# One build-time schedule for all five engines in a chunk-selecting attention followed by a softplus MLP

## Chip, cores and metric

One core of one Trainium2 chip runs the whole kernel. The metric is device time in microseconds (us) of one execution, as the median of several runs. The core has a matrix engine (PE, with its weight loads shown apart as PEld), a vector engine (DVE), an activation engine (ACT), a general engine (POOL) and a queue engine (SP) that issues transfers. Each engine takes its instructions strictly in the order in which they stand in its queue and waits on semaphores for what other engines or transfers must deliver.

## What is computed

```python
B, H, S, D = 4, 8, 768, 64;  chunk = 32;  nc = 24;  top_k = 6
k_min, k_max = min and max of k over each chunk of 32 keys
ub = sum_d max(q * k_min, q * k_max)            # a bound per query and chunk
ub = where(pos // 32 >= chunk index, ub, -1e9)  # causal, by chunks
sel = the 6 chunks with the largest ub of each query
scores = where(sel and causal, q @ k.T / 8, -1e9)
attn = softmax(scores) @ v                      # (4, 8, 768, 64) -> x: (3072, 512)
h = x @ w_in                                    # 512 -> 2048
g = softplus(h)
out = g @ w_out                                 # 2048 -> 512, float32
```

Inputs are float32; the kernel computes in bfloat16 with float32 accumulation.

## The kernel before

The 3072 rows are cut into 12 **blocks** of 256 queries, three to a batch (block kinds 0, 1 and 2: a block of kind k sees k + 1 key spans of 256). For each block there are two stages.

*Preparation* (`prep_block`): k and q of the block are transposed on PE (L175, L191), ACT copies the transposed k out of PSUM into `kt` (L179), DVE reduces `kt` to chunk maxima and minima (`kx`, L181 and L182) and spreads them into a block-diagonal matrix `bd` (L184). DVE makes the positive and negative parts `qpos`, `qneg` of q (L203, L204); PE multiplies both by `bd` (`ub`, L212, L213, always all 24 chunks), DVE adds a causal mask over all 24 chunks (L217), takes the 8 largest of each of 16 rows (L224), compares with the sixth (`mraw`, L226) and PE transposes the result (`mT`, L236, eight transposes, one for each head pair and half block). The mask rows are copied into spare rows of the operands `qa` and `qt` (L241 to L245), and k into `ka` and `kb` (L197, L198 or L239, L240, from `kt`), so that one score matmul yields score plus mask.

*Attention and MLP*: for each of 4 head pairs, `score_step` makes score tiles `s_ps` (two matmuls, L263 and L265), ACT takes the exponential into `pt` (L267), POOL cuts the diagonal (L271); `av_step` multiplies by v (`o_ps`, L285), DVE normalises (L291, L293); `ot_step` transposes into `x` (L304, L305). Then `h_gen`: 64 matmuls `hp` with w_in (L322) with Exp and Ln on ACT (L324, L326), and `y_gen`: 32 matmuls `y` with w_out (L335), a copy on DVE (L340) and a store on SP (L342).

The order is written out by hand: `run_block` steps through the score tiles of a block, and after each tile `slot` runs pieces of the older attention steps, of the MLP (`mlp_stream`, at a rate per slot), of the next block's preparation (the `agenda`: five pieces at slots 0, 2, 5, 9 and 11 of 16) and of the loads. PSUM is cut into pools: two banks for `s_ps`, one for `o_ps`, two for all transposes and `ub`, two for `hp`, one for `y`.

Loads: the k, q, v of blocks 0 to 2 come as float32 (`load_f32`, queues of SP and, for half of block 0, ACT) and are cast on ACT (L103). From block 3 on POOL's queue casts them in the transfer (`load_cast`, L108, L114). The loads of blocks 0, 1 and 2 are issued one behind the other; w_in is issued on POOL's queue in eight pieces (two column halves by four row blocks, L149) during block 0's score tiles, w_out in four pieces behind it (L155).

```python
    with tc.manual_schedule(engines={ET.Activation, ET.DVE, ET.PE}):
        consts(0)
        ...
        loads.append(load_w_in())
        run_block(0, 0.0)
    for nm in "kqv":
        load_f32(nm, 2, (nc.sync, nc.sync))
    consts(1)
    loads.append(load_w_out())
    run_block(1, 0.8)
```

Of the kernel before, what the change touches and what calls it, by code (L numbers as in the profile page):

```python
# [16 lines left out]


@with_exitstack
def kernel(  # L20
# [9 lines left out]
    nc = tc.nc  # L30
    B, H, S, D = q.shape
    CH = 32
    NCH = S // CH
    TOPK = 6
    NQT = S // 128
    NP = H // 2
    scale = 1.0 / math.sqrt(D)
    NEG = -30000.0 / scale

    d_model, d_ff = moe_w_in.shape  # L40
    KDM = d_model // 128
    KFF = d_ff // 128
    QB = 256
    NT = QB // 128
    NBLK = S // QB
    NCB = QB // CH
    blocks = [(b, blk) for b in range(B) for blk in range(NBLK)]
    NB = len(blocks)

    ctx.enter_context(tc.manual_schedule(engines={ET.Pool, ET.SP}))  # L50
    nc.scalar.preload_act_table_set("natural_log_exp_and_others")

    PS = bass.MemoryType.PSUM
    singles = ctx.enter_context(tc.tile_pool(name="singles", bufs=1))
    f_pool = ctx.enter_context(tc.tile_pool(name="f", bufs=6))
    io_pool = ctx.enter_context(tc.tile_pool(name="io", bufs=3))
    qt_pool = ctx.enter_context(tc.tile_pool(name="qt", bufs=3))
    prep = ctx.enter_context(tc.tile_pool(name="prep", bufs=2))
    pt_pool = ctx.enter_context(tc.tile_pool(name="pt", bufs=3))
    st_pool = ctx.enter_context(tc.tile_pool(name="st", bufs=3))  # L60
    x_pool = ctx.enter_context(tc.tile_pool(name="x", bufs=4))
    g_pool = ctx.enter_context(tc.tile_pool(name="g", bufs=3))
    e_pool = ctx.enter_context(tc.tile_pool(name="e", bufs=3))
    mo_pool = ctx.enter_context(tc.tile_pool(name="mo", bufs=3))
    ps_s = ctx.enter_context(tc.tile_pool(name="ps_s", bufs=2, space=PS))
    ps_o = ctx.enter_context(tc.tile_pool(name="ps_o", bufs=1, space=PS))
    ps_t = ctx.enter_context(tc.tile_pool(name="ps_t", bufs=2, space=PS))
    ps_h = ctx.enter_context(tc.tile_pool(name="ps_h", bufs=2, space=PS))
    ps_y = ctx.enter_context(tc.tile_pool(name="ps_y", bufs=1, space=PS))

    V = [singles.tile([128, NQT, H, D + 1], BF16, name=f"v_{i}") for i in range(2)]
    KA = [singles.tile([128, NP, S], BF16, name=f"ka_{i}") for i in range(2)]
    KB = [singles.tile([128, NP, S], BF16, name=f"kb_{i}") for i in range(2)]
    BD = [singles.tile([128, NP, 2, 2, NCH], BF16, name=f"bd_{i}") for i in range(2)]
    Mraw = [singles.tile([128, NP, NT, 2, 32], BF16, name=f"mraw_{i}") for i in range(2)]
    w_in_sb = singles.tile([128, KDM, d_ff], BF16, name="w_in_sb")
    w_out_sb = singles.tile([128, KFF, d_model], BF16, name="w_out_sb")

    src = {"k": k, "q": q, "v": v}
    xfs, loaded = {}, {}  # L80

    def rows(nm, n, t):
        b, blk = blocks[n]
        r0 = blk * QB + t * 128
        return src[nm][b, :, r0:r0 + 128].rearrange("h s d -> s h d")

    def load_f32(nm, n, eng):
        xf = f_pool.tile([128, NT, H, D], F32, name="xf")
        for t in range(NT):
            eng[t].dma_start(out=xf[:, t], in_=rows(nm, n, t))  # L90
        xfs[nm, n] = xf

    def v_dst(n, t):
        b, blk = blocks[n]
        return V[b % 2][:, blk * NT + t, :, 0:D]

    def cast_f32(nm, n):
        xf = xfs.pop((nm, n))
        if nm != "v":
            loaded[nm, n] = io_pool.tile([128, NT, H, D], BF16, name=nm + "_sb")  # L100
        for t in range(NT):
            dst = v_dst(n, t) if nm == "v" else loaded[nm, n][:, t]
            nc.scalar.copy(dst, xf[:, t])  # L103

    def load_cast(nm, n):
        if nm == "v":
            for t in range(NT):
                nc.gpsimd.dma_start(out=v_dst(n, t), in_=rows(nm, n, t))  # L108
                yield
        else:  # L110
            xb = io_pool.tile([128, NT, H, D], BF16, name=nm + "_sb")
            loaded[nm, n] = xb
            for t in range(NT):
                nc.gpsimd.dma_start(out=xb[:, t], in_=rows(nm, n, t))  # L114
                yield

    for nm in "kqv":
        load_f32(nm, 0, (nc.sync, nc.scalar))

    ident = singles.tile([128, 128], BF16)  # L120
    make_identity(nc, ident)
    ohb = singles.tile([32, S], BF16, name="ohb")
    nc.vector.memset(ohb, NEG)
    cmask = singles.tile([128, NQT, NCH], F32, name="cmask")
    nc.vector.memset(cmask, 0.0)
    nc.gpsimd.affine_select(out=ohb, in_=ohb, compare_op=ALU.is_ge, fill=0.0,
                            base=0, channel_multiplier=-CH, pattern=[[1, S]])
    nc.gpsimd.affine_select(out=ohb, in_=ohb, compare_op=ALU.is_ge, fill=0.0,
                            base=CH - 1, channel_multiplier=CH, pattern=[[-1, S]])
    nc.gpsimd.affine_select(out=ohb, in_=ohb, compare_op=ALU.not_equal, fill=-1.0,  # L130
                            base=-NCH, channel_multiplier=1, pattern=[[0, S]])
    nc.gpsimd.affine_select(out=cmask, in_=cmask, compare_op=ALU.is_ge, fill=-1.0e30,
                            base=0, channel_multiplier=1, pattern=[[128, NQT], [-CH, NCH]])

    for i in range(2):
        nc.vector.memset(Mraw[i], 0.0)

    def consts(i):
        nc.vector.memset(BD[i], 0.0)
        nc.vector.memset(KB[i][0:32], 0.0)  # L140
        nc.vector.memset(V[i][:, :, :, D:D + 1], 1.0)
        nc.sync.dma_start(out=KA[i][64:96], in_=ohb.unsqueeze(1).to_broadcast([32, NP, S]))
        nc.sync.dma_start(out=KB[i][32:64], in_=ohb.unsqueeze(1).to_broadcast([32, NP, S]))

    def load_w_in():
        for half in range(2):
            fs = slice(half * d_ff // 2, (half + 1) * d_ff // 2)
            for kt in range(KDM):
                nc.gpsimd.dma_start(out=w_in_sb[:, kt, fs],  # L149
                                    in_=moe_w_in[kt * 128:(kt + 1) * 128, fs])  # L150
                yield

    def load_w_out():
        for c4 in range(4):
            nc.gpsimd.dma_start(  # L155
                out=w_out_sb[:, c4 * 4:(c4 + 1) * 4, :],
                in_=moe_w_out[c4 * 512:(c4 + 1) * 512, :].rearrange(
                    "(kt ki) f -> ki kt f", ki=128))
            yield

    Q = {}

    def prep_block(n):
        b, blk = blocks[n]
        ka, kb, bd = KA[b % 2], KB[b % 2], BD[b % 2]
        mraw = Mraw[n % 2]
        cs = slice(blk * QB, (blk + 1) * QB)
        cc = slice(blk * NCB, (blk + 1) * NCB)
        early = n < NBLK
        k_sb = loaded.pop(("k", n))  # L170

        kT = ps_t.tile([128, NP, QB], BF16, name="kT", tag="t")
        for t in range(NT):
            for p in range(NP):
                nc.tensor.transpose(kT[:, p, t * 128:(t + 1) * 128],  # L175
                                    k_sb[:, t, 2 * p:2 * p + 2, :], ident)
        kx = prep.tile([128, NP, 2, NCB], BF16, name="kx")
        kt = prep.tile([128, NP, QB], BF16, name="kt")
        nc.scalar.copy(kt, kT)  # L179
        kT4 = kt.rearrange("d p (c g) -> d p c g", g=CH)  # L180
        nc.vector.tensor_reduce(kx[:, :, 0], kT4, axis=AX.X, op=ALU.max)  # L181
        nc.vector.tensor_reduce(kx[:, :, 1], kT4, axis=AX.X, op=ALU.min)  # L182
        for h in range(2):
            nc.vector.tensor_copy(bd[h * 64:(h + 1) * 64, :, :, h, cc], kx[h * 64:(h + 1) * 64])  # L184
        yield

        q_sb = loaded.pop(("q", n))
        qT = ps_t.tile([128, NP, QB], BF16, name="qT", tag="t")
        for t in range(NT):
            for p in range(NP):  # L190
                nc.tensor.transpose(qT[:, p, t * 128:(t + 1) * 128],  # L191
                                    q_sb[:, t, 2 * p:2 * p + 2, :], ident)
        qt = qt_pool.tile([128, NP, QB], BF16, name="qt")
        qa = qt_pool.tile([128, NP, QB], BF16, name="qa")
# [26 lines left out]
        for p in range(NP):  # L221
            for t in range(NT):
                for h in range(2):
                    nc.vector.max(out=m8[:, p, t, h], in_=ub_sb[:, p, t, h])  # L224
# [262 lines left out]
```

## Time and profile before

| | |
|---|---|
| time, 3 runs | 315.68, 315.86, 316.93 us, median 315.86 |
| span of the profiled execution, first to last instruction | 314.1 us |
| the median less that span (start and end of a launch) | 1.8 us |
| busy: PE / PEld / DVE / ACT / POOL | 270.5 / 198.6 / 174.4 / 224.2 / 99.0 us |
| mean granted PE clock | 0.988 |
| moved by DMA | 23.51 MB, mean 75 GB/s |

The page gives no time of its own for the profiled execution besides its span. Busy time is the union of the spans of an engine's instructions. A matmul's span holds the time from its start to its last result, while the next one may start long before, so a row of back-to-back matmuls is read from the starts. In a row of the windows view, the first two numbers are the stretch, then come its length and for each engine the busy time with the number of instructions, the granted PE clock, the mean busy share of the DMA engines, and GB/s.

### The profile page before, as it was taken

How to read it: one execution, taken by the hardware profiler on the slowest of the kernel's cores; microseconds unless marked ns; L12 is line 12 of the kernel's file. 1: busy time of each engine (PE TensorE's matmuls, PEld its weight loads, DVE VectorE, ACT ScalarE, POOL GpSimd, SP SyncE). 2: the span in 40 equal slices, each digit the busy share in tenths (PEclk: the TensorE clock that was granted, in tenths of full speed). 3: DMA queues.
4: the chain of work that ended last, by engine and by line, in shares of the span. 5: the costliest groups of instructions: out<-in, count | busy, mean ns of one | idle time of the engine just before them, and what ended most of it. 6: DMA issues, size and time to landing. Idle time of an engine off the chain costs nothing.

```text
span 314.1 us, 6878 instructions
## 1 busy us (share of the span) xinstructions
PE 270.5 (86%) x2748; PEld 198.6 (63%) x2784; DVE 174.4 (56%) x550; ACT 224.2 (71%) x379; POOL 99.0 (32%) x172
## 2 busy tenths in 40 slices
PE   1335879989899799899999799899999999999983
PEld 0223657667658667677658577677568777776651
DVE  5818582592965964935946946836748732112100
ACT  4578789968837858788628868888539769983550
POOL 4024375622723613514624414424421211111000
PEclk9999959999999999999999999999999999999999
DMA  9999899993933906904913905907900000001101
GB/s 165 200 216 216 147 158 189 92 71 45 80 73 52 83 11 60 101 2 57 90 59 53 83 35 33 102 3 76 94 33 35 3 33 35 2 33 35 67 17 52
DMA packets 82208, 23.51 MB, mean 75 GB/s; under 512 B 75520, under 2 KB 78080, under 8 KB 82176
## 3 DMA queue, kind: packets, MB, share of 16 engines
q0 software_dynamic: 59424, 11.28, 43.9%
q1 hardware_dynamic: 19632, 11.01, 14.3%
q10 hardware_dynamic: 3120, 0.79, 1.4%
q8 instruction: 21, 0.34, 0.4%
q14 instruction: 11, 0.09, 0.1%
HBM read 27.26 MB, written 6.29 MB: 107 GB/s over the span
## 4 chain that ended last, share of the span: by engine, by line
PE 57%; DVE 26%; ACT 12%; issue 2%; DMA 1%; ACTq 0%; DVEq 0%
PE y L335 21%; PE hp L322 17%; PE o_ps L285 5%; PE s_ps L263 4%; DVE kx L181 4%; ACT kt L179 4%; DVE kx L182 4%; PE s_ps L265 3%; PE mT L236 3%; ACT pt L267 2%; DVE qneg L204 2%; ACT e_sb L324 2%; DVE qpos L203 2%; DVE qt L200 2%; DMA xf<-in_k_dram 1%
## 5 line engine op out<-in xcount | busy, mean ns | idle before, releaser
L267 ACT ACTIVATE pt<-s_ps 128x512 bf16<-128x512 f32 (+1 forms) x192 | 103.9, 556 | 36.7 <-PE s_ps L265 29.9
L322 PE MATMUL hp<-x,w_in_sb 128*128 128x256 bf16 x768 | 103.5, 273 | 3.2 <-ACT e_sb L324 1.8
L271 POOL TENSOR_SCALAR_AFFINE_SELECT pt<-pt 128x256 bf16<-128x256 bf16 x96 | 40.9, 426 | 185.5 <-ACT pt L267 185.1
L335 PE MATMUL y<-w_out_sb,g 128*128 128x512 bf16 x348 | 90.7, 379 | 3.6 <-DVE y_sb L340 1.7
L322 PEld LDWEIGHTS <-w_in_sb 128*128 128x128 bf16 x768 | 71.4, 98 | 12.9 <-issue 4.1
L324 ACT ACTIVATE e_sb<-hp 128x512 f32<-128x512 f32 x96 | 58.4, 611 | 27.7 <-PE hp L322 27.4
L335 PEld LDWEIGHTS <-g 128*128 128x128 bf16 x384 | 34.2, 97 | 28.6 <-issue 2.8
L326 ACT ACTIVATE g<-e_sb 128x1024 bf16<-128x1024 f32 x48 | 51.8, 1078 | 0.3
L285 PEld LDWEIGHTS <-pt 128*128 128x128 bf16 x672 | 32.9, 99 | 11.1 <-issue 4.3
L340 DVE COPY y_sb<-y 128x512 f32<-128x512 f32 x24 | 16.5, 687 | 39.7 <-PE y L335 39.5
L291 DVE RECIPROCAL rec<-o_ps 128x4 f32<-128x4 f32 x48 | 8.5, 177 | 38.1 <-PE o_ps L285 37.9
L305 DVE COPY x<-oT 128x256 bf16<-128x256 bf16 x48 | 13.9, 289 | 25.1 <-PE oT L304 24.8
L285 PE MATMUL o_ps<-v_106,pt 128*128 128x65 bf16 x336 | 20.7, 199 | 2.2 <-DVE o_sb L293 1.9
L181 DVE TENSOR_REDUCE kx<-kt 128x32 bf16<-128x1024 bf16 x12 | 14.6, 1219 | 13.0 <-ACT kt L179 13.0
L293 DVE TENSOR_TENSOR o_sb<-o_ps,rec 128x256 bf16<-128x256 f32 x48 | 20.2, 422 | 1.3
L285 PE MATMUL o_ps<-v_107,pt 128*128 128x65 bf16 x336 | 18.4, 193 | 1.7 <-DVE o_sb L293 1.5
L304 PE MATMUL oT<-ident,o_sb 128*128 128x128 bf16 x96 | 13.7, 225 | 4.3 <-DVE o_sb L293 4.3
L114 POOL DMA_DIRECT2D k_sb<-in_k_dram x18 | 16.1, 892 | 0.8 <-issue 0.5
L114 POOL DMA_DIRECT2D q_sb<-in_q_dram x18 | 16.2, 902 | 0.4 <-issue 0.3
L175 PE MATMUL kT<-ident,k_sb 128*128 128x128 bf16 x96 | 8.8, 241 | 8.1 <-ACT k_sb L103 7.6
L263 PE MATMUL s_ps<-qt,kb_110 128*128 128x256 bf16 x48 | 14.0, 293 | 1.6 <-ACT pt L267 0.9
L263 PE MATMUL s_ps<-qa,ka_108 96*128 96x256 bf16 x48 | 14.2, 296 | 0.8 <-DVE qa L241 0.8
(111 smaller groups left out, 365.2 us busy)
## 6 DMA issues: line engine op xcount, KB each, us to landing
out_dram<-y_sb SPq DMA_DIRECT2D x24, 256.0 KB, 2.0
k_sb<-in_k_dram POOLq DMA_DIRECT2D x18, 128.0 KB, 3.8
q_sb<-in_q_dram POOLq DMA_DIRECT2D x18, 128.0 KB, 4.3
w_in_sb<-in_moe_w_in_dram POOLq DMA_DIRECT2D x8, 256.0 KB, 6.9
w_out_sb<-in_moe_w_out_dram POOLq DMA_DIRECT2D x4, 512.0 KB, 9.5
v_107<-in_v_dram POOLq DMA_DIRECT2D x12, 128.0 KB, 5.3
xf<-in_k_dram SPq DMA_DIRECT2D x5, 256.0 KB, 5.1
xf<-in_q_dram SPq DMA_DIRECT2D x5, 256.0 KB, 5.8
```

The costliest lines, as they stand in the source:

```text
L114: nc.gpsimd.dma_start(out=xb[:, t], in_=rows(nm, n, t))
L181: nc.vector.tensor_reduce(kx[:, :, 0], kT4, axis=AX.X, op=ALU.max)
L263: nc.tensor.matmul(s_ps[:, 0:QB], kk[0:nr, p, j * 128:(j + 1) * 128], qq[0:nr, p, :], start=True, stop=True)
L267: nc.scalar.activation(pt[:, h, j:j + 2].rearrange("k j c -> k (j c)")[:, 0:w], s_ps[:, 0:w], ACT.Exp, scale=scale)
L271: nc.gpsimd.affine_select(out=diag, in_=diag, compare_op=ALU.is_ge, fill=0.0, base=0, channel_multiplier=-1, pattern=[[0, 2], [1, 128]])
L285: nc.tensor.matmul(o_ps[:, u, h], pt[:, h, j, c0:c0 + 128], V[b % 2][:, j, 2 * p + h, :], start=(j == 0), stop=(j == t0 + u))
L293: nc.vector.tensor_tensor(o_sb, o_ps[:, :, :, 0:D], rec.to_broadcast([128, NT, 2, D]), op=ALU.mult)
L322: nc.tensor.matmul(hp[:, fi], w_in_sb[:, dt, ft * 128:(ft + 1) * 128], X[n][:, dt], start=(dt == 0), stop=(dt == KDM - 1))
L324: nc.scalar.activation(e_sb[:, f2 * 2:f2 * 2 + 2], hp, ACT.Exp)
L326: nc.scalar.activation(g[:, f4 * 4:(f4 + 1) * 4], e_sb, ACT.Ln, bias=1.0)
L335: nc.tensor.matmul(y, g[:, f, u * 128:(u + 1) * 128], w_out_sb[:, f, :], start=(f == 0), stop=(f == KFF - 1))
L340: nc.vector.tensor_copy(y_sb, y)
```

## The change

The hand-written order is replaced by a graph of operations. Each operation has an engine (some have two to choose from, with a price in ns for each), what it depends on, the buffers that it takes and frees, a due time (`key`), and for loads an earliest time (`rel`) and a `gate`: another transfer that must have landed before it is issued. `Plan.run` simulates the five engines when the kernel is built and places, one after the other, the operation that can start first; among those that can start at the same time on an engine (within `tol` ns) the one with the earliest due time. The order found is then the program order of all five engines, all of which now stand under the manual schedule. The simulation's prices are formulas in the file (`mm`, `act`, `dve`, `LAT`).

With it:
- buffers are single tiles with fixed places that the planner hands out (`sizes`); PSUM has the same eight banks as before, but the transposes of the first two blocks may also take the banks of `h` and `y`;
- w_in is loaded in four column pieces of 512 columns (1 MB of float32 each) gated on the landing of block 1's v; block 2's float32 loads are gated on the third of these pieces, w_out on block 2's v, and everything that comes later on the last piece of w_out; all of the first float32 loads are on SP's queue;
- `ub` has only the 8(k + 1) chunks that a block of kind k can see; the causal mask is added in place, in PSUM, on the four chunks on the diagonal alone; the 8 largest are taken straight from PSUM over those chunks; `mT` takes two head pairs in one transpose (four instead of eight for a block);
- `kt` is gone: DVE reduces the transposed k straight from PSUM, and `ka`, `kb` are copied from PSUM too;
- the minima are negated, so that both parts of q are non-negative; this may run on ACT (Relu);
- blocks 0 and 1 are prepared in two halves of two head pairs each;
- the zeroed rows of the second `kb` and the mask rows of the second `ka`, `kb` come by DMA behind w_out.

The matmuls of scores, v, `hp` and `y` are the same in number and shape. The diff's core (the constants, the operation class, and all code of operations that only changes its form are left out):

```diff
+LAT = {
+    "PE": {"PE": 230, "ACT": 205, "DVE": 205},
+    "ACT": {"PE": 165, "ACT": 145, "DVE": 145, "POOL": 180, "SP": 200},
...
+    def run(self, par):
+        for o in reversed(self.ops):
+            dur = min(c for _, c in o.alts) + (2500 if o.dma else 160)
+            o.due = min([1e12 if o.key is None else o.key] + [s.due - dur for s in o.succ])
+        free = {"PE": 3000.0, "ACT": 2300.0, "DVE": 1000.0, "POOL": 800.0, "SP": 800.0}
...
+            for e, v in cand.items():
+                lim = min(x[0] for x in v) + tol.get(e, 0)
+                x = min((x for x in v if x[0] <= lim), key=lambda x: (x[1].due, x[0], x[1].n))
+                if pick is None or (x[0], x[1].due) < (pick[0], pick[1].due):
+                    pick = (*x, e)
...
+def mm(n):
+    return max(25.0, n / 2.4 + 2.5)
+def act(n, psum=True):
+    return n / 1.2 + (52 if psum else 95)
+def dve(n, rate=1.0):
+    return n / (0.96 * rate) + 66
+PAR = dict(
+    tol={"PE": 1, "ACT": 46, "DVE": 0, "POOL": 0, "SP": 0},
+    alt=39,
...
+    sizes=dict(s=2, h=2, y=1, o=1, t=2, xf=10, io=4, kx=2, q=3, pn=2, ub=2, pt=2, osb=2, x=4, g=3, e=2, ysb=2),
+)
...
+    for i, nm in enumerate("kqv"):
+        load(nm, 0, "f32", 0.1 + 0.6 * i)
+    for i, nm in enumerate("kqv"):
+        load(nm, 1, "f32", 2.0 + 0.6 * i)
+    load_w_in(5.0, [ld["dma", "v", 1, 0]])
+    for i, nm in enumerate("kqv"):
+        load(nm, 2, "f32", 9.0 + 0.6 * i, gate=[w_in[2]])
+    load_w_out(14.0, [ld["dma", "v", 2, 0]])
...
+            def f_kx(e, kT=kT, kx=kx, pp=pp, j=0, t_of=t_of):
+                x = t_of(kT).rearrange("d p (c g) -> d p c g", g=CH)
+                nc.vector.tensor_reduce(kx.ap[:, pp, j], x, axis=AX.X, op=ALU.min if j else ALU.max, negate=bool(j))
...
+                    copy(e, (T.KB if h else T.KA)[i][hs, pp, cs], t_of(kT)[hs])
...
+            C = NCB * (k + 1)
...
+                            nc.vector.max(out=ubs.ap[:, p // 2, t, p % 2, h], in_=x[:, (p - p0) // 2, t, p % 2, h, 0:c])
...
+    need = mybir.DependencyInfo(mybir.DependencyClass.Sync, mybir.DependencyReason.DATA)
+    for o in order:
+        o.inst = o.fn(o.eng)
+        for d in o.gate:
+            tc.add_manual_dep(o.inst.ins, d.inst.ins.name, need, reason="order of loads")
...
-    with tc.manual_schedule(engines={ET.Activation, ET.DVE, ET.PE}):
-        consts(0)
...
-    while later:
-        slot(1.0)
-    for _ in mlp:
-        pass
```

More of the change, by code (lines that the diff above doesn't have):

```diff
@@ new lines, with __init__, ap @@
+LANDED = {"PE": 60, "ACT": 40, "DVE": 40, "POOL": 80, "SP": 80}
+class Pool:
+    def __init__(self, n):
+        self.homes = [None] * n
+        self.ends = [[] for _ in range(n)]
+        self.idle = list(range(n))
+class Buf:
+    __slots__ = ("pools", "pool", "slot", "left", "ends")
+    def __init__(self, *pools):
+        self.pools, self.pool, self.slot, self.left, self.ends = pools, None, None, 0, []
+    @property
+    def ap(self):
+        return self.pool.homes[self.slot]
+class Op:
+    __slots__ = ("name", "alts", "fn", "deps", "gate", "after", "succ", "alloc", "touch", "key",
+                 "rel", "due", "wait", "eng", "start", "end", "done", "dma", "n", "at", "inst")
@@ L77 @@
[L77 to L91, printed above, removed]
```

891 lines of the change are left out of this document (527 added, 364 removed).

## The prediction

> **What bounds the kernel now.** I read the page first (busy times, groups), then PE's timeline for the true spacing of its matmuls, then the windows view to see where PE does less than it could.
>
> ```profile
> PE 270.5 (86%) x2748; PEld 198.6 (63%) x2784; DVE 174.4 (56%) x550; ACT 224.2 (71%) x379; POOL 99.0 (32%) x172
> ...
> L267 ACT ACTIVATE pt<-s_ps 128x512 bf16<-128x512 f32 (+1 forms) x192 | 103.9, 556 | 36.7 <-PE s_ps L265 29.9
> L322 PE MATMUL hp<-x,w_in_sb 128*128 128x256 bf16 x768 | 103.5, 273 | 3.2 <-ACT e_sb L324 1.8
> L335 PEld LDWEIGHTS <-g 128*128 128x128 bf16 x384 | 34.2, 97 | 28.6 <-issue 2.8
> L285 PEld LDWEIGHTS <-pt 128*128 128x128 bf16 x672 | 32.9, 99 | 11.1 <-issue 4.3
> ```
>
> PE is the busiest engine, but 270.5 us counts overlapping spans. PE's timeline gives the spacing from start to start:
>
> ```profile
> 80.32 0.46 PE L285 MATMUL o_ps<-v_106,pt 128*128 128x65 bf16 x10
> 80.62 1.04 PE L322 MATMUL hp<-x,w_in_sb 128*128 128x256 bf16 x8
> ...
> 272.17 1.03 PE L335 MATMUL y<-w_out_sb,g 128*128 128x512 bf16 x4
> 273.03 0.27 PE L263 MATMUL s_ps<-qa,ka_109 96*128 96x256 bf16 x1
> 273.14 0.27 PE L265 MATMUL s_ps<-qa,ka_109 96*128 96x256 bf16 x1
> 273.25 1.04 PE L322 MATMUL hp<-x,w_in_sb 128*128 128x256 bf16 x8
> 274.13 0.27 PE L263 MATMUL s_ps<-qa,ka_109 96*128 96x256 bf16 x1
> 274.24 0.22 PE L265 MATMUL s_ps<-qa,ka_109 96*128 96x128 bf16 x1
> 274.30 0.46 PE L285 MATMUL o_ps<-v_107,pt 128*128 128x65 bf16 x10
> ```
>
> Four `y` in 0.86 us are 215 ns each; eight `hp` in 0.88 are 110; a 128-column matmul takes 60 (I use 56, half of 110); ten `o_ps` in 0.30 are 30. The work is then `hp` 768 x 109 ns = 83.7 us, `y` 384 x 215 = 82.6, scores (two for each of 192 exponentials, 96 of the 384 with 128 columns) 288 x 109 + 96 x 56 = 36.8, `o_ps` 672 x 30 = 20.2. Of the 2784 loads 576 remain: 384 transposes x 56 = 21.5 and 192 bounds of 48 columns, which lie by their columns (21) and the 30 of `o_ps` at some 25 each, 4.8. Together **249.6 us of work in a span of 314.1**: 64.5 us are lost, not the 43.6 that the busy time suggests. (The Trainium skill, "Perfetto Trace Analysis", section Identifying the Most-Contended Engine, calls matmul busy time a bad measure of distance to the limit because matmuls are pipelined; the trace agrees, 270.5 against 249.6.)
>
> Where they are lost, by windows (the last three rows are those of `hp`, `y` and `s_ps` alone):
>
> ```profile
> 60.00:308.70 248.70, 234.52 (x2397) 171.44 (x2429) 140.31 (x433) 178.37 (x307) 75.05 (x126) 1.00 0.46 50
> 60.00:70.00 10.00, 8.60 (x95) 5.92 (x94) 9.78 (x36) 6.91 (x13) 4.82 (x7) 1.00 0.89 57
> 80.00:90.00 10.00, 8.33 (x102) 5.81 (x102) 9.16 (x34) 6.35 (x12) 5.59 (x9) 1.00 1.12 94
> 270.00:300.00 30.00, 29.69 (x261) 20.67 (x264) 5.48 (x14) 19.92 (x34) 2.04 (x5) 1.00 0.10 36
> 0.00:60.00 60.00, 9.59 (x64) 6.22 (x64) 0.94 1.23 180
> 0.00:60.00 60.00, 0.70 (x3) 0.39 (x4) 0.94 1.23 180
> 0.00:60.00 60.00, 12.63 (x56) 0.94 1.23 180
> ```
>
> By 60 us PE has done one block's `hp` (7.0 us), four `y` (0.9), blocks 0 and 1 of attention and part of block 2. A block's attention work with its preparation, by the same spacings, is 4.0, 6.7 and 9.4 us for kinds 0, 1, 2. So some 22 us are done: 38 us lost. From 60 to 308.7 the other 227.5 fill 91.5% of 248.7: 21 us lost. The tail loses 5.4. The middle loss sits where DVE is full: in 60:70 and 80:90 DVE is busy 9.78 and 9.16 of 10 and PE 8.60 and 8.33; with no preparation left (270:300) PE is busy 29.69 of 30.
>
> **The start.** Loads bind it:
>
> ```profile
> 0.00:20.00 20.00, 5.36 (x44) 3.41 (x44) 11.67 (x38) 10.50 (x15) 3.68 (x11) 1.00 1.15 190
> ```
> ```profile
> k_sb<-in_k_dram POOLq DMA_DIRECT2D x18, 128.0 KB, 3.8
> ```
> ```profile
> L322 PE MATMUL hp<-x,w_in_sb x768: 269/272/421, 35.7 to 301.0; 128*128 128x256 bf16 x192
> L335 PE MATMUL y<-w_out_sb,g x348: 376/379/390, 58.6 to 308.3; 128*128 128x512 bf16 x174
> ```
>
> The core moves 190 GB/s. Blocks 0 and 1 are twelve pieces of 256 KB; eleven and the mask rows, about 3.2 MB, land at 17 to 18 us. Then the gate opens: a 128 KB transfer by POOL's queue lands after 3.8 us, of which 0.7 is moving at that rate, so 3.1 is delay; a column piece (512 KB as stored) takes 2.7. The pieces land at about 23, 26, 28.5 and 31. One column piece is enough for the first `hp`, where before one needed a half of w_in: `hp` starts at 23 instead of 35.7. Block 2 follows the third piece; its fifth piece lands at about 36, so w_out's pieces land from 42 to 50, and `y` can start at **42** instead of 58.6. Of PE's work, before 42 there are block 0 (4.0), block 1 (6.7) and two `hp` blocks (14.0), at most 24.7. I take 22, since block 1's exponentials hold back the second `hp`; the low end is 18. From 42 on, block 2's attention, two blocks of `y` and the next `hp` are at hand, so PE is full 18 us earlier with the same work done.
>
> The gates are waits. Behind a gated load on POOL's queue stand diagonal cuts of block 0 and 1, for which `o_ps` waits; the planner knows the wait and sorts by it, so I price this at nothing; if POOL were stuck until a gate opens, block 0's `x` would slip by up to 3 us, still before 23. The casts of blocks 1 and 2 lie beside PE's waiting.
>
> **The parts that change work.** `mT` loses 48 of 96 transposes, 2.7 us of PE: 247.0 remain. DVE, in order:
>
> ```profile
> 80.75 0.68 DVE L200 COPY qt<-qT 128x1024 bf16<-128x1024 bf16 x1
> ...
> 84.42 0.17 DVE L291 RECIPROCAL rec<-o_ps 128x4 f32<-128x4 f32 x1
> 84.51 0.39 DVE L239 COPY ka_109<-kt 64x1024 bf16<-64x1024 bf16 x1
> ...
> 86.26 1.44 DVE L224 MAX8 m_1307<-ub_sb 128x8 f32<-128x24 f32 x16
> ```
>
> `ka` and `kb` cost 0.39 us from SBUF; from PSUM the nearest row is the 0.68 of `qt`: 2 x 0.29 us more in each of nine blocks, 5 us of DVE time beside PE. (The Trainium skill, "VectorE: DVE Perf Modes", section Why PSUM operands drop a tier, says that a PSUM operand keeps DVE out of its fastest copies. It speaks against this edit, and 0.39 against 0.68 agrees.) The sixteen maxima from PSUM are not in the trace: they cost 1.44 us a block now; if each cost as much as the small PSUM read of 0.17, 2.7; if shorter rows halve them, 0.7. I keep 1.44, the same operation. The mask on four chunks instead of 24 saves DVE a little, and ACT loses its copies `kt`. So DVE's work stays near 15 us a block (174.4 / 12 now) against 20.6 of PE (247.0 / 12); what changes is when it is done. Now the five pieces are packed into 12 of 16 slots and fill DVE, so that `o_ps` and `y` (one bank each) wait for their copies. The planner places each operation where it can start and prefers what is due, so most of the 21 us should go. Between 91.5% and the 99% of 270:300 I take 97%, nearer to the latter, because `y` and `hp` of an older block are then ready to fill in, and because two slow DVE steps a block remain.
>
> **The tail** is the same work:
>
> ```profile
> 305.10 3.61 PE L335 MATMUL y<-w_out_sb,g 128*128 128x512 bf16 x16 [0.78 <-DVE y_sb L340]
> 308.75 0.69 DVE L340 COPY y_sb<-y 128x512 f32<-128x512 f32 x1 [3.70 <-PE y L335]
> ```
>
> From PE's end at 308.7 to 314.1 are 5.4 us.
>
> **Sum.** 42 + (247 - 22) / 0.97 + 5.4 = 42 + 232 + 5.4 = 279.4 us of span, against 314.1. The median lies 1.8 us above the span: **281 us**. With 18 us of work by 42 and 95% it is 290; with 24.7 and 99%, 274: the forecast's own range.
>
> **Rivals.** *The DVE bursts stay* (inputs land late before each block, so its preparation is still a burst; the PSUM copies lengthen it): 91.5% after 42 gives 246 and 295 us. For it: DVE's work does not shrink. Against: DVE idles 44% of the span, and a block's 15 us need only be spread over its 20.6.
>
> *The array stays slow at the start.*
>
> ```profile
> 21.57 0.42 PE L263 MATMUL s_ps<-qa,ka_108 96*128 96x256 bf16 x1
> ...
> 37.90 0.27 PE L263 MATMUL s_ps<-qt,kb_110 128*128 128x256 bf16 x1
> ```
> ```profile
> 40.50:47.30 6.80, 5.99 (x53) 4.40 (x54) 5.48 (x28) 5.71 (x12) 4.97 (x8) 0.50 1.08 158
> ```
>
> The same matmul spans 0.42 us at 21.6 and 0.27 at 37.9, and from 40.5 to 47.3 the granted clock is 0.50. If waits for column pieces keep it at half until 42, the 14 us of `hp` need 28, some 7 us less is done by 42, and 288 results. (The Trainium skill, "TensorE: Matmul & The Clock Gate", Part 1, says that an array idle for about 3.4 us drops to half rate and needs as long of work to rise. By that rule the dense `hp` from 23 us would cost 3 us only; the drop at 40.5 behind sparse work fits it.)
>
> *The gates do not hold the order* (they wait for the issue alone): w_in moves in among block 1's pieces, block 1 comes some 8 us later, 4 us less is done: 285.
>
> *Slower: every hand-over is planned too early.* An order fixed for just-in-time arrivals stalls PE wherever the real one is later. There are 288 PSUM tiles that ACT must free (192 `pt`, 96 `e_sb`). The plan prices a `pt` at 425 ns on average, the page shows 556: 131 ns each are 38 us, against the 35 gained; at 150 ns it is 281 + 43 = 324. The point at which it decides is 120 ns. Against it: the plan adds 165 ns from ACT's end to PE's start, 590 in all, so the page's 556 is already covered.
>
> **How the numbers follow.** Forecast 0.64, bursts 0.14, slow array 0.10, gates 0.04: all faster, 0.92. Planned too early 0.06 slower, and 0.02 for a price that just eats the gain. About 0.5% (1.6 us) is what this kernel's measurement can tell from no change. The range, 271 to 297, takes in the forecast's 274 to 290 and the first three rivals, and leaves out about 0.15.
>
> **What would show it.** Right: first `hp` near 23, first `y` near 42, no ten-microsecond window after 50 with PE under 9.3, DVE never full for ten. Wrong: `y` first near 50 or later; PE idle under `e_sb`, `pt` or `o_sb` by over 10 us in sum; granted clock 0.5 beyond 30 us.

## The result and the profile after

The changed kernel takes 296.16 us (median of four runs, 295.73 to 296.55) against 315.91 us for the kernel before on the same chip: a ratio of 0.935, 95% interval 0.931 to 0.939. The profiled execution has a span of 294.1 us and a time of 295.79. In the new kernel `ph`, `py`, `ps`, `po` are the PSUM tiles that were `hp`, `y`, `s_ps` and `o_ps`, `pt` is both the tile of exponentials and the PSUM tile of transposes, and every copy stands on L224 (ACT) or L225 (DVE).

The page of the changed kernel, engine totals and the costliest group:

```profile
PE 264.2 (90%) x2736; PEld 194.7 (66%) x2736; DVE 154.0 (52%) x538; ACT 230.4 (78%) x417; POOL 98.0 (33%) x176
...
L544 ACT ACTIVATE pt<-ps 128x512 bf16<-128x512 f32 (+1 forms) x192 | 96.6, 552 | 15.7 <-PE ps L538 14.9
```

PE's work is what the prediction counted (247.0 us: the matmuls of the changed kernel at the prediction's spacings). What PE waits for, from the view of waits, the longest rows (us in total, times, longest):

```profile
PE pt L383 <- ACT io L224: 4.9, 1, 4.9
PE ps L536 <- ACT pt L544: 4.3, 6, 0.9
PE pt L584 <- DVE osb L576: 2.4, 6, 0.6
PE pt L383 <- DVE kb L225: 2.1, 1, 2.1
PE ps L536 <- DVE qa L225: 2.0, 2, 1.2
```

The first row is the start, until the first load is there and cast. The rest are few places, and with the two smaller rows of the same tiles (0.8 and 1.2) `pt` and `osb` come to 8.7 us, under the 10 named as a sign of being wrong. The start, from the views of the tiles `w_in_sb`, `py` and `w_out_sb` (first and last start at the end of each row):

```profile
L608 PE MATMUL ph<-x,w_in_sb x768: 269/273/421, 28.0 to 281.9; 128*128 128x256 bf16 x192
L627 PE MATMUL py<-w_out_sb,g x384: 376/379/389, 49.7 to 289.7; 128*128 128x512 bf16 x192
L324 POOL DMA_DIRECT2D w_out_sb<-in_moe_w_out_dram x4: 750/766/899, 41.7 to 44.1; - x4
```

The first `hp` comes at 28.0, not 23, and the first `y` at 49.7, not 42; "`y` first near 50 or later" was another of the signs of being wrong. The windows view (same columns as in the prediction):

```profile
20.00:30.00 10.00, 6.49 (x59) 4.62 (x57) 7.46 (x41) 7.13 (x17) 2.86 (x6) 1.00 1.13 178
30.00:40.00 10.00, 9.91 (x123) 8.71 (x122) 3.62 (x12) 9.47 (x19) 1.99 (x5) 1.00 0.87 159
40.00:50.00 10.00, 7.01 (x84) 5.72 (x80) 8.25 (x26) 7.39 (x14) 3.87 (x6) 0.83 0.75 115
50.00:60.00 10.00, 9.02 (x74) 6.79 (x72) 2.47 (x15) 9.00 (x15) 2.47 (x4) 1.00 0.87 154
80.00:90.00 10.00, 8.92 (x96) 7.32 (x97) 6.73 (x19) 8.61 (x17) 2.46 (x7) 1.00 0.24 37
60.00:270.00 210.00, 203.43 (x2217) 151.50 (x2216) 115.57 (x386) 173.47 (x319) 77.66 (x131) 1.00 0.61 60
```

DVE, full for 9.78 and 9.16 us of 10 in 60:70 and 80:90 before, is at 6.73 in 80:90, and in no stretch of ten after 60 above 8.93: the bursts are gone. What is not gone is a weak stretch from 40 to 60, and windows like 80:90 (8.92, where the prediction wanted 9.3 everywhere after 50).

The clock of 1.00 in the row 20:30 must be read with care. The trace's clock records begin at 31.3 us, with 1.00, and the view prints 1.00 for all that lies before. PE's spacing says otherwise: the first eight `hp`, issued from 28.04 to 29.75, stand 214 ns apart, against 110 later. So the clock was at half until 31.3. The next record of half clock is from 45.0 to 48.4.

**The account.** I count PE's work done by a given moment from the matmuls issued, each at the spacing that the prediction used. Every row below comes from that count; "share" is the work left at 60 us over the time from 60 to PE's end.

| kernel | done by 40 | done by 60 | PE's end | share after 60 |
|---|---|---|---|---|
| prediction's sum | – | 39.5 | 274.0 | 97% |
| changed kernel | 15.9 | 29.7 | 290.1 | 94.4% |
| raised DVE prices (e9) | 16.5 | 29.3 | 285.5 | 96.5% |
| the same, cold clock in the plan (e10) | 16.5 | 31.5 | 284.3 | 96.1% |
| e9's prices, filler, new keys (e12) | 14.4 | 28.4 | 284.5 | 97.4% |

The changed kernel's span is 14.7 us above the sum: 9.8 us less work is done by 60 (10.1 us at 97%), 94.4% instead of 97% costs 230.1 - 217.3 / 0.97 = 6.1, and the tail is 1.4 shorter. The last copy went from DVE at 0.69 us (the prediction's row at 308.75) to ACT at 0.59, and the rest is the end of the last store, 4.0 us behind PE's end instead of 5.4.

```profile
290.11 0.59 ACT L224 COPY ysb<-py 128x512 f32<-128x512 f32 x1 [3.70 <-PE py L627]
```

**Plan against chip.** The order comes from a simulation whose own times can be printed when the kernel is built, so each matmul of the trace can be set beside the moment at which the plan expected it. The difference, in us:

| plan's time | 23 | 34 | 45 | 56 | 88 | 119 | 152 | 183 | 215 | 237 | 267 |
|---|---|---|---|---|---|---|---|---|---|---|---|
| chip later by | 4.6 | 6.2 | 7.3 | 8.4 | 10.4 | 11.8 | 13.8 | 15.4 | 17.7 | 19.2 | 19.2 |

The plan ends at 273.9. It slips 8.4 us in the start, then about 1.2 us with each block, and from the moment at which the last block is prepared it slips no more, although scores, exponentials, `y` and their copies go on. So what is planned too early lies in the preparation, or in what runs only while blocks are still prepared, such as the loads. Its steps on DVE, by form, after:

```profile
L225 DVE COPY kb<-pt 64x1024 bf16<-64x1024 bf16 x10 | 6.9, 694 | 0.5 <-ACT ka L224 0.3
L225 DVE COPY ka<-pt 64x1024 bf16<-64x1024 bf16 x9 | 6.1, 681 | 0.1
L225 DVE COPY qa<-qt 64x1024 bf16<-64x1024 bf16 x10 | 6.0, 601 | 0.0
L432 DVE TENSOR_SCALAR qpos<-qt 128x1024 bf16<-128x1024 bf16 x9 | 4.6, 507 | 0.2
L392 DVE TENSOR_REDUCE kx<-pt 128x32 bf16<-128x1024 bf16 x20 | 23.6, 1220 | 9.6 <-PE pt L383 9.6
```

The plan prices the first four at 599, 599, 353 and 363 ns. The two small copies that make `bd` are priced at 180 ns together and take 360 to 510 from the first's start to the second's end; each half of the mask rows' copy is priced at 695 and takes about 860. The largest fit: the maxima and minima `kx` are priced at 1133 and stand 1140 apart.

A span is not yet a price, since on DVE too the next instruction can start before a span has ended: `kx` spans 1220 and stands 1140 from the next. From start to start `kb` takes 725 ns, `ka` 608 to 715, and `qpos` 332 where nothing stretches it (less than its price) and 670 in its two longest. Counted in that way for all of DVE's preparation of blocks 3 to 11 (to the next start where that follows at once, else to the own end), a block takes 1.36 us more than planned, beside a slip of 1.2.

One way by which this reaches PE can be read at the start of a block (rows of one stretch of the timeline, with others between):

```profile
178.75 1.17 ACT L224 COPY qt<-pt 32x512 bf16<-32x512 bf16 x2 [0.65 <-DVE qa L225]
...
181.02 0.98 ACT L544 ACTIVATE pt<-ps 128x512 bf16<-128x512 f32 x2
181.67 0.27 PE L536 MATMUL ps<-qt,kb 128*128 128x256 bf16 x1 [0.89 <-ACT pt L544]
```

ACT stands still for DVE's copy of the mask rows, so its exponentials come later, and PE waits for a free score bank. From 60 to 270 us ACT waits 4.6 us at that place in the changed kernel, 3.8 in e3 and 2.7 in e9.

### The profile page after: what moved, and what is told of

It is laid out like the page before. It is cut to its first block, busy times and chain, and to the rows that moved or that the text cites. A ratio compares the mean times of both kernels' runs of the same rounds, so it can differ in the third digit from the quotient of the medians.

```text
span 294.1 us, 6913 instructions
## 1 busy us (share of the span) xinstructions
PE 264.2 (90%) x2736; PEld 194.7 (66%) x2736; DVE 154.0 (52%) x538; ACT 230.4 (78%) x417; POOL 98.0 (33%) x176
## 4 chain that ended last, share of the span: by engine, by line
PE 57%; DVE 20%; ACT 17%; issue 3%; DMA 1%; SPq 0%; ACTq 0%; DVEq 0%
PE ph L608 19%; PE py L627 19%; PE ps L536 5%; DVE kx L392 5%; ACT pt L544 5%; ACT g L618 5%; PE po L566 5%; ACT qt L224 4%; PE ps L538 4%; DVE qa L225 3%; DVE osb L576 2%; PE pt L383 2%; ACT e L613 2%; DVE kb L225 2%; PE pt L584 2%
## 5 line engine op out<-in xcount | busy, mean ns | idle before, releaser
L544 ACT ACTIVATE pt<-ps 128x512 bf16<-128x512 f32 (+1 forms) x192 | 96.6, 552 | 15.7 <-PE ps L538 14.9
L608 PE MATMUL ph<-x,w_in_sb 128*128 128x256 bf16 x768 | 100.5, 276 | 0.2
L627 PE MATMUL py<-w_out_sb,g 128*128 128x512 bf16 x384 | 96.4, 379 | 1.7 <-ACT g L618 1.0
L613 ACT ACTIVATE e<-ph 128x512 f32<-128x512 f32 x96 | 57.5, 610 | 16.4 <-PE ph L608 15.5
L618 ACT ACTIVATE g<-e 128x1024 bf16<-128x1024 f32 x48 | 51.2, 1066 | 0.6
L392 DVE TENSOR_REDUCE kx<-pt 128x32 bf16<-128x1024 bf16 (+1 forms) x26 | 27.6, 1097 | 10.1 <-PE pt L383 10.1
L566 PE MATMUL po<-v,pt 128*128 128x65 bf16 x672 | 29.0, 195 | 2.0 <-DVE osb L576 1.2
L536 PE MATMUL ps<-qt,kb 128*128 128x256 bf16 x96 | 26.5, 281 | 4.1 <-ACT pt L544 4.1
L536 PE MATMUL ps<-qa,ka 96*128 96x256 bf16 x96 | 26.4, 281 | 2.4 <-DVE qa L225 2.0
L538 PE MATMUL ps<-qt,kb 128*128 128x128 bf16 (+1 forms) x96 | 23.8, 251 | 0.0
L383 PEld LDWEIGHTS <-io 128*128 128x128 bf16 x192 | 14.4, 106 | 12.5 <-ACT io L224 5.9
L225 DVE COPY ysb<-py 128x512 f32<-128x512 f32 x9 | 6.2, 692 | 23.9 <-PE py L627 23.8
L224 ACT COPY ysb<-py 128x512 f32<-128x512 f32 x15 | 8.8, 585 | 11.4 <-PE py L627 11.0
```

The lines of the kernel that those rows point to most:

```text
L383: nc.tensor.transpose(o[:, p - p0, t * 128:(t + 1) * 128], SBt[nm, n].ap[:, t, 2 * p:2 * p + 2, :], T.ident)
L392: nc.vector.tensor_reduce(kx.ap[:, pp, j], x, axis=AX.X, op=ALU.min if j else ALU.max, negate=bool(j))
L536: nc.tensor.matmul(sp.ap[:, 0:QB], kk[0:nr, p, j * 128:(j + 1) * 128], qq[0:nr, p, :], start=True, stop=True)
L538: nc.tensor.matmul(sp.ap[:, QB:w], kk[0:nr, p, (j + 1) * 128:(j + 2) * 128], qq[0:nr, p, 128 if last else 0:], start=True, stop=True)
L544: lambda e, sp=sp, pt=pt, h=h, j=j, w=w: nc.scalar.activation(pt.ap[:, h, j:j + 2].rearrange("k j c -> k (j c)")[:, 0:w], sp.ap[:, 0:w], A ...
L566: nc.tensor.matmul(o[:, u, h], pt.ap[:, h, j, c0:c0 + 128], T.V[i][:, j, 2 * p + h, :], start=(j == 0), stop=(j == t0 + u))
```

## Experiments

Each ran beside the kernel before on one chip (three chips in all), with medians of 315.9 to 316.8 us for that kernel. Ratios are to that kernel, with 95% intervals; the changed kernel stands at 0.935 (0.931 to 0.939).

**e1: w_out issued earlier.**

```diff
-    load_w_out(14.0, [ld["dma", "v", 2, 0]])
+    load_w_out(14.0, [ld["dma", "k", 2, 0]])
```

> Theory: in the changed kernel w_out is issued at 41.7 us although its gate (block 2's fifth piece) opened at 37.1, since it stands behind late diagonal cuts on POOL; with the gate on block 2's first piece (landed at 32.1) it is issued near 37, first y near 45 instead of 49.7, time 293 us (-3). The plan itself ends 1.5 us later, so the slip of the chip against the plan's end falls from 20.2 to about 16. Rival (the start is late only because PE runs at half clock): first y moves, time stays within 1 us of 296.

Measured: 296.69 us, 0.937 (0.933 to 0.940). The gate's piece of v landed at 37.1 in the changed kernel, but POOL, in order, was behind a diagonal cut that waited for ACT:

```profile
40.97 0.79 POOL L554 TENSOR_SCALAR_AFFINE_SELECT pt<-pt 128x256 bf16<-128x256 bf16 x2 [2.40 <-ACT pt L544]
...
41.71 3.13 POOL L324 DMA_DIRECT2D w_out_sb<-in_moe_w_out_dram  x4
```

The plan of e1 ends 1.5 us later than that of the changed kernel, and the slip to the end of the span is 19.6 us (20.2 there), not the 16 expected. The transfers are issued from 38.2 on, 3.5 us earlier, and the first `y` is still at 50.4. w_out's landing isn't what holds it; the same 2.1 us hole is there, for block 2's k:

```profile
38.20 3.21 POOL L324 DMA_DIRECT2D w_out_sb<-in_moe_w_out_dram  x4
...
44.33 0.69 DVE L225 COPY kb<-pt 64x1024 bf16<-64x1024 bf16 x1 [0.25 <-ACT ka L224]
45.08 1.01 PE L383 MATMUL pt<-ident,io 128*128 128x128 bf16 x8 [2.11 <-DVE kb L225]
...
50.44 1.03 PE L627 MATMUL py<-w_out_sb,g 128*128 128x512 bf16 x2
```

**e2: PE kept busy from the start,** by 64 groups of four 128-column matmuls into the bank of `y`, which the early transposes then may not use.

```diff
+    def f_fill(e):
+        for _ in range(4):
+            nc.tensor.matmul(pool["y"].homes[0][:, 0:128], T.ident, T.ident, start=True, stop=True)
+    for r in range(NFILL):
+        P.op("fill", [("PE", 4 * mm(128))], f_fill, [ident])
-            also = [pool["h"], pool["y"]] if n < 2 else []
+            also = [pool["h"]] if n < 2 else []
```

> 64 groups of four idle 128-column matmuls into the y bank fill PE's gaps of the first 25 us. Theory: half clock until 31 us costs the changed kernel 6 us against its plan; filled, PE reaches full rate by about 10 us, first hp comes at 25 or earlier instead of 28.0, and the slip against the plan at the first hp falls from 4.6 to 2 or less. The plan with the filling ends 3.2 us later (277.1 against 273.9), so 293 to 294 us if nothing else changes. Rival (transfers or hand-overs bind the start): first hp stays at 28, time 299.

Measured: 296.38 us, 0.936 (0.932 to 0.939). The clock is full from 7.3 us on (31.3 in the changed kernel), and at half again from 44.9 to 48.3. The first `hp` comes at 27.3, not at 25 or earlier. The chip's slip at plan time 56 falls from 8.4 to 6.1: by that the half clock of the first 31 us costs 2.3 us there. (Each slip is measured against the run's own plan, and the later half clock is in both.) The plan itself ends 3.2 later (277.1), with one bank less for the early transposes, and that takes it back. 30.0 us of work are done by 60, as without it.

**e3: three DVE prices raised** (`qpos` and `qneg` by 120 ns, `qa` by 240, `mraw` by 100, for a whole block); the work stays, but the planner may change the order, and the engine of an operation that has two.

```diff
-  [("DVE", dve(L * QB, 4) + 30), ...          # qpos, qneg
+  [("DVE", dve(L * QB, 4) + 30 + EXTRA[0] * L), ...
-  [("DVE", dve(L * QB, 4) + 20)], ...         # qa
+  [("DVE", dve(L * QB, 4) + 20 + EXTRA[1] * L)], ...
-  [("DVE", dve(L * 4 * C) + 160)], f_raw
+  [("DVE", dve(L * 4 * C) + 160 + EXTRA[2])], f_raw
```

> Order alone changes: the planner prices DVE's copies between SBUF tiles as the chip showed them (qpos/qneg +120 ns, qa +240, mraw +100). Theory: after 60 us the chip loses 11 us against the plan because these copies take longer than planned; planned truly (plan's end 275.8, +1.9) the loss falls to 6 or less and the time to 292 or 293. Rival: the loss after 60 us comes from elsewhere and stays 11: 298.

Measured: 292.13 us, 0.921 (0.917 to 0.925): 4 us faster with the same work; 3 instructions fewer on DVE and 3 more on ACT. The slip goes from 9.3 at plan time 56 to 13.4 at the end: 4.1 us lost behind the start instead of 10.8. The plan ends 1.9 us later and the chip 3.5 earlier.

**e4: no loads on POOL's queue for blocks 3 to 11.** Their place is taken by one-column transfers on SP's queue.

```diff
-  o = P.op(f"ld {nm}{n}.{t}", [("POOL", 890)],
-           lambda e, t=t: nc.gpsimd.dma_start(out=into(nm, n, t), in_=rows(nm, n, t)),
+  o = P.op(f"ld {nm}{n}.{t}", [("SP", 450)],
+           lambda e, t=t: nc.sync.dma_start(out=into(nm, n, t)[:, 0, 0:1], in_=T.ident[:, 0:1]),
```

> Leaves out the loads of blocks 3 to 11 (a transfer of one column by SP's queue stands in for each; POOL issues none of them). Theory: POOL's issuing stretches DVE's copies; without it qa takes about 430 ns instead of 601 and qpos 430 instead of 507, and the loss against the plan after 60 us falls from 11 to 5 or 6: 291 us with a plan that ends 1.5 us later. Rival (the diagonal cuts or something else stretch them): durations stay, time 296 to 298.

The kernel leaves the loads out, so both the issuing on POOL and the transferred data are gone. It tests why the copies are long. In the changed kernel's timeline they lie beside POOL's issuing:

```profile
151.07 1.93 POOL L297 DMA_DIRECT2D io<-in_k_dram  x2
151.44 0.75 DVE L432 TENSOR_SCALAR qpos<-qt 128x1024 bf16<-128x1024 bf16 x1
...
152.44 0.78 DVE L225 COPY qa<-qt 64x1024 bf16<-64x1024 bf16 x1
```

Measured: 296.12 us, 0.936 (0.932 to 0.940). The copies do get short, by form:

```profile
L225 DVE COPY qa<-qt 64x1024 bf16<-64x1024 bf16 x10 | 4.3, 432 | 0.0
L432 DVE TENSOR_SCALAR qpos<-qt 128x1024 bf16<-128x1024 bf16 x10 | 4.2, 423 | 0.2
```

601 became 432 and 507 became 423. The trace of the changed kernel has the same split within it: the six `qa` that overlap an issue on POOL average 692 ns, the other four 465. But the slip behind the start is still 8.9 us. My theory, that POOL's issuing is the main cause of the loss, falls: it is some 2 of the 11 us. The rest is there with quiet copies too, in steps that are priced too low whatever POOL does.

**e9: DVE prices as measured without POOL's loads.** `bd` 430 (350 for a half), `ka` and `kb` + 95 each, the mask sum + 100, the sixteen maxima 88 each, `mraw` + 70, `qa` + 75 (428, e4's figure, not 601), the mask rows' copies + 170; `qpos` and `qneg` stay.

```diff
-  [("DVE", 180 if L == 4 else 160)], f_bd
+  [("DVE", 430 if L == 4 else 350)], f_bd
-  alts = [("DVE", dve(L * QB, 2))]            # ka, kb
+  alts = [("DVE", dve(L * QB, 2) + 95)]
...
-  alts = [("DVE", 2 * dve(L // 2 * QB, 2) + 30), ...   # mask rows
+  alts = [("DVE", 2 * dve(L // 2 * QB, 2) + 200), ...
```

> Order alone changes. Theory: the changed kernel's loss of 11 us against its plan after 56 us comes mostly from DVE steps of the preparation that the plan prices too low even without POOL's interference (bd 180 against 370 to 510 ns on the chip, mask copies 695 against 870, ka/kb 599 against 695, mask sum 319 against 430, qa 353 against 425 and more), about 1.2 us a block, each passed on to PE. With these prices the plan ends at 276.4 (+2.4); the loss after 56 us falls to 3 us or less, so 290 to 291 us. Rival (the slack matters, not the prices: the loss is in the hand-overs between engines): loss stays near 11, 298 us.

Measured: 292.06 us, 0.924 (0.920 to 0.927). The slip behind the start falls to 4.9 us (7.3 to 12.2), and PE's share after 60 rises from 94.4% to 96.5%. Here 12 instructions move from DVE to ACT (busy 147.4 and 237.3 us, against 154.0 and 230.4), so it is not the order alone.

e3 and e9 raise steps that are only in part the same, and gain the same. What counts seems to be the sum: counted as above, a block's preparation on DVE takes 1.36 us more than planned in the changed kernel, 1.05 in e4, 0.38 in e3 (where the raised steps now take less than planned and the others more) and 0.19 in e9. The slip behind the start is 1.20, 0.99, 0.46 and 0.54 us a block. So a remainder of about 0.5 a block does not come from these prices. A plan with the same sum added in the wrong place was not tried.

Against the windows of the changed kernel the early one is no better, the long one is:

```profile
40.00:50.00 10.00, 6.93 (x69) 4.61 (x67) 8.36 (x35) 8.37 (x13) 4.24 (x6) 0.86 0.78 115
50.00:60.00 10.00, 8.96 (x88) 6.85 (x87) 0.84 (x2) 8.22 (x15) 3.58 (x6) 0.97 0.78 133
60.00:270.00 210.00, 206.29 (x2236) 155.13 (x2235) 110.11 (x379) 181.91 (x331) 76.43 (x129) 1.00 0.62 63
```

**e10: e9, and PE at 1.95 times its price until 30 us,** so that the plan knows of the half clock.

```diff
+                    if e == "PE" and t < par["cold"]:
+                        c *= 1.95
```

> As the run with the true DVE prices, and the planner also prices PE at 1.95 times until 30 us, which is where the granted clock rose in the changed kernel. Order alone changes. Theory: 6 to 8 us of slip up to the first y come from the half clock; planned for, the slip at y falls from 7 or 8 to 3 us or less; the plan ends at 279.3, so the time is 279.3 + 3 + 3 + 1.7 = 287, some 3 us below the run with true DVE prices alone. Rival: the clock costs the time whatever the order, so the same time as that run within 1 us.

Measured: 291.72 us, 0.922 (0.918 to 0.925), the same as e9. The slip at plan time 57 is now 3.2 and at the end 8.0, so the plan describes the chip better, and the first `y` is at 44.5; but the plan ends at 279.3, 2.9 later than e9's. Knowing the cold clock does not give its time back.

**e6: all 24 chunks again** for the bounds, the mask and the maxima.

```diff
-            C = NCB * (k + 1)
+            C = NCH
```

> Undoes the bounds over causal chunks: all 24 chunks, causal mask over all of them, maxima over 24. More DVE work in blocks of kinds 0 and 1 (mask sum, comparison), no PE work of note. Theory (PE's slip comes from DVE's preparation steps): slower by 1 to 3 us, 297 to 299, DVE busy some 3 to 6 us more. Rival (this part is off the path): within 1 us of 296.

Measured: 300.39 us, 0.950 (0.947 to 0.954): the causal-chunk bounds are worth about 4.2 us, more than I expected. DVE is busy 159.4 us instead of 154.0, and the slip behind the start grows from 10.8 to 12.8.

**e7: only w_in's four column pieces, in the kernel before.**

```diff
-        for half in range(2):
-            fs = slice(half * d_ff // 2, (half + 1) * d_ff // 2)
-            for kt in range(KDM):
-                nc.gpsimd.dma_start(out=w_in_sb[:, kt, fs], in_=moe_w_in[kt * 128:(kt + 1) * 128, fs])
+        for c in range(4):
+            fs = slice(c * d_ff // 4, (c + 1) * d_ff // 4)
+            nc.gpsimd.dma_start(out=w_in_sb[:, :, fs], in_=moe_w_in[:, fs].rearrange("(kt ki) f -> ki kt f", ki=128))
```

> The kernel before with w_in loaded in four column pieces at the same place in its order: one part of the change alone. Theory (the start gains from the order of the loads and of the engines, not from the shape of the pieces): first hp stays within 1.5 us of 35.7 because block 0's x is ready only then, and the time within 1.5 us of 316. Rival (hp waits for half of w_in): first hp comes 4 to 6 us earlier and the time falls by 3 to 5 us.

Measured: 314.73 us against 316.46, 0.993 (0.991 to 0.996). The first `hp` moves from 35.7 to 35.3 only, so the prediction's reason for the late `hp`, that it needs a half of w_in, was wrong.

**e11: the reverse, eight half-pieces in the changed kernel,** gated as before on block 1's v (block 2's loads on the sixth piece).

```diff
-        for c in range(4):
+        for c in range(8):
...
+                kt, fs = c % 4, slice(c // 4 * FF // 2, (c // 4 + 1) * FF // 2)
```

> Undoes w_in by columns: eight pieces as in the kernel before (two column halves by four row blocks), the same gates, block 2 behind the sixth. Theory: first hp waits for block 0's x (28.0 in the changed kernel), and the first half of w_in lands near 27, so little changes: first hp at 28 to 30, time within 1.5 us of 296. Rival (the column pieces carry the earlier start): first hp 3 us or more later and 299 us.

Measured: 294.05 us, 0.930 (0.925 to 0.935): not slower; the intervals meet. The first `hp` is at 29.7, 1.7 later. Neither way do the column pieces carry the early start.

**e12 and e13: e9's prices with due times searched anew** for the earliest planned end, e12 with 56 filler groups as well.

```diff
-    tol={"PE": 1, "ACT": 46, ...},  att=(3.5, 3.5, 8.7),  av=-4.26,  ot=-1.32,  hlag=3.01, ...
+    tol={"PE": 1, "ACT": 54.26, ...},  att=(3.7, 3.5, 6.31),  av=-6.15,  ot=-3.09,  hlag=6.0, ...   # e12
+    att=(3.26, 2.81, 8.61),  mlp=14.8,  av=-5.6,  ot=0.83,  hlag=0.39, ...                         # e13
```

> True DVE prices, 56 groups of idle matmuls in PE's early gaps, and due times searched anew for the earliest end of the plan (273.8). Theory: the slips are additive: 5 us at the start with a warm PE, 5 us after 56 us with true prices, so 273.8 + 10 + 1.7 = 285.5, faster than every kernel so far. Rival (what is taken from the slip comes back as a later plan or in waits, as in the runs with the filling and with the cold price): 290 to 292.

> True DVE prices and due times searched anew (the plan ends at 273.5), no filling. Theory: the slip of the run with true prices stays (13 us, 7 at the start and 5 after), so 273.5 + 13 + 1.7 = 288. Rival (a plan searched to be tighter leaves less slack, so the chip slips more): 290 or more.

Measured: e12 289.51 us, 0.914 (0.908 to 0.920); e13 289.98, 0.917 (0.912 to 0.922), where 285.5 and 288 were expected. They are the two fastest, and their intervals overlap. The plans end at 273.8 and 273.5, 2.6 and 2.9 earlier than e9's; the chip gains 2.6 and 2.1. In e12 PE's share after 60 reaches 97.4%, yet only 28.4 us are done by then. Filling did not hold the clock there: it is at half from 27.6 to 34.4 and from 48.0 to 51.5.

**e14: e9 and e4 together.**

> Leaves out the loads of blocks 3 to 11 (a transfer of one column by SP's queue stands in for each) with the true DVE prices. Theory: what is left of the loss after 56 us with true prices (4.9 us) is POOL's issuing, which stretches DVE's copies; without it the loss is 2 us or less, and the time some 2 to 3 us below the run with true prices alone, corrected for the plan's own end. Rival (the rest lies in hand-overs): the loss stays near 5.

Measured: 293.66 us, 0.929 (0.925 to 0.933), no better than e9, with a plan that ends 1.8 us later. The slip behind the start is 5 to 6 us, as with POOL's loads (4.9). The stretched copies are not what is left of it.

## Why the prediction was right in sign and too good by 15 us

The measured 296 us lies above the sum's own 274 to 290; only the width that the rivals gave to the stated range takes it in.

**Right.** The loss was bubbles, and they were at the two places named: windows with DVE full, and the first 60 us. The first are nearly gone. That is not by order alone, because DVE's work did not stay near 15 us a block, as the prediction had it: its busy time fell from 174.4 to 154.0 us, 15 of the 24 copies of `y` and 19 of the 48 of `x` having gone to ACT, and part of the bounds having gone altogether (e6). PE's matmuls are as counted. The maxima from PSUM cost about what they cost from SBUF: sixteen take 1.50 us below (1.37 in blocks of kind 1), against 1.44, and `ka` and `kb` from PSUM the 0.68 that was forecast.

```profile
49.47 1.50 DVE L473 MAX8 ub<-pt 128x8 f32<-128x20 f32 x16
```

**The first failed step: "PE is full 18 us earlier", from 42 on, with 22 us done.** It took two landings for two starts. By 42 us 17.6 us are done, below the low end of 18 too. The first piece of w_in did land early (21.7 us, against 23), but the last copy of block 0's `x` ends at 26.2, and in PE's order `hp` stands behind block 1's first scores, which wait 1.24 us for mask rows out of a bank that `hp` needs as well:

```profile
25.85 0.37 ACT L224 COPY x<-pt 128x256 bf16<-128x256 bf16 x1 [0.26 <-PE pt L584]
...
27.01 0.60 DVE L225 COPY qa<-ph 32x256 bf16<-32x256 bf16 x2 [0.88 <-ACT qt L224]
27.34 0.37 PE L536 MATMUL ps<-qa,ka 96*128 96x256 bf16 x1 [1.24 <-DVE qa L225]
...
28.04 0.63 PE L608 MATMUL ph<-x,w_in_sb 128*128 128x256 bf16 x2
```

And that block 2's attention is "at hand" from 42 on forgot that it needs its whole preparation, in order, on engines that are still busy with block 1. Its k landed at 32.1 and was cast at 38.44, behind block 1's `x` on DVE; the PSUM tile of its k came free with `kb` at 45.3; its first scores stand at 54.2. In the changed kernel:

```profile
38.23 0.29 DVE L225 COPY x<-pt 128x256 bf16<-128x256 bf16 x1 [0.68 <-PE pt L584]
38.44 0.75 DVE L225 CAST io<-xf 128x512 bf16<-128x512 f32 x2
...
44.63 0.69 DVE L225 COPY kb<-pt 64x1024 bf16<-64x1024 bf16 x1 [0.34 <-ACT ka L224]
...
45.38 1.01 PE L383 MATMUL pt<-ident,io 128*128 128x128 bf16 x8 [2.09 <-DVE kb L225]
...
54.24 0.27 PE L536 MATMUL ps<-qa,ka 96*128 96x256 bf16 x1
```

Between 40 and 54 PE has little but `hp` and the first `y` to do. That this chain is the bound of the start is read from the trace, not shown: what the runs show is that w_out earlier (e1), a full clock (e2) and a plan that knows the cold clock (e10) each leave the work done by 60 at 28.9 to 31.5 us. Bringing block 2's loads or casts forward was not tried.

**The gates priced at nothing** were a miss of detail: w_out was issued 4.6 us behind the landing that opened its gate, since POOL stood in front of a cut. By e1 issuing it 3.5 us earlier gains nothing here, but not for the reason I gave (that the planner sorts by it).

**The second failed step: 97%.** It is 94.4%. I had allowed for "two slow DVE steps a block" that PE would hardly feel. In fact the plan's prices for a block's preparation are too low by 1.2 to 1.4 us (the slip, and the count above), and an order fixed for those prices passes the delay on to PE. e3 and e9 show it: changed prices, with the order and engines that follow from them, bring 4 us and 96.5%.

**The rivals.** *The slow array* came true as an observation, and past the point that I had named (half clock until 31.3 us, again from 45.0 to 48.4), but its price was smaller: I had given 7 us to a half clock until 42, e2 shows 2.3 for one until 31.3. (The estimate of 3 us that the prediction worked out by the rule of the Trainium skill, "TensorE: Matmul & The Clock Gate", Part 1, was nearer.) The clock's fall at 45.0 stands near the end of the 2.1 us hole (43.3 to 45.4), and in the 3.4 us before it PE was busy 0.92. In the kernel before, PE was busy 1.97 of the 3.4 us ahead of the fall at 40.5. (By the same page of the Trainium skill a fall takes about 3.4 us of idleness; in both kernels the clock fell behind less.) So the prediction's remark that the drop at 40.5 fits that rule does not hold to the letter. *Every hand-over planned too early* is refuted in the form in which I put it: 24 of the 192 exponentials and 18 of the 96 `e` start behind the last preparation, which at the rival's 131 ns each would make 5.5 us, and there the plan slips 0.1. A small part of its thought, order fixed for hand-overs that come late, was right for one family of steps, and it took away 6 us, not 43. *DVE bursts stay* is refuted by the windows. *Gates that do not hold*: block 2's pieces land from 32.1 on, behind w_in's third at 28.7, as meant.

**Of the 19.7 us gained,** 4.2 belong to the causal-chunk bounds (e6), and the column pieces are worth 1.7 us in the kernel before (e7) and cost 2.1 in the changed one (e11), where the intervals meet. That the remaining 15 or so are the order is what is left over; it was not undone by itself, and `mT`'s 2.7 us and the work moved from DVE to ACT are in it.

**Still open:** the last 6 us of slip in the start, with the clock full (e2); the 4 to 6 us behind the start that are left in e3, e9 and e14; and why plans with a tighter end slip more (15.1 and 15.8 us to the end of the span in e12 and e13 against 13.1 in e9), so that 289.5 stands where 285.5 was expected. In e12 all of that lies in the start: the slip at plan time 56 is 9.4 us (8.7 in e13, 7.3 in e9), and behind it 4.3 (5.9 and 4.9).

## What to carry to other kernels

When an order is fixed when the kernel is built, compare the plan's own times with the trace and look where the difference grows: a slope points to one family of steps with wrong prices, a jump to a wait, and a flat stretch speaks for the prices of what runs in it. Price each instruction of an operation, in the place where it will run, before moving anything; here changed prices brought 4 us. And a transfer that lands early is a start only if nothing else is missing: follow every input of the first big matmul, and of the next block, through each engine's queue.

## What the runs showed of the hardware

In this case a DVE copy from SBUF to SBUF takes longer with loads on POOL's queue than without: 601 against 432 ns for `qa`, 507 against 423 for `qpos` (means of nine or ten, changed kernel against e4), with single ones up to 790; the copies from PSUM, `ka` and `kb`, do not (681 and 694 against 683 and 694). In the changed kernel the clock was at half until 31.3, 3.3 us behind the first of the dense `hp`; with 128-column filler matmuls it was full at 7.3 (e2).
